# Attention and MoE on one core: where the loads of v stand in the queue, and which pairs take k and v in runs

## The chip, the cores and the metric

One core of one Trainium2 chip (trn2) runs the whole program. The metric is the device time of one execution in microseconds (us). The times of a kernel are the median of several executions; the profile is one further execution, taken by the hardware profiler.

## The reference

The kernel computes an attention layer and feeds its output to a feed-forward layer with a gate (called MoE below). q, k and v are float32 of shape (4, 8, 576, 64): batch, heads, tokens, head dimension.

```python
q_rot, k_rot = rotate(q), rotate(k)            # rotary embedding, halves of 32
scores = q_rot @ k_rot.T / sqrt(64)
attn = exp(scores - max) / (sum + 1e-9)
x = attn @ v                                   # to (4, 576, 512)
h = relu(x @ w_in)                             # 512 -> 1024
gate = sigmoid(conv over tokens of h, 3 taps)  # per channel
out = (h * gate) @ w_out                       # 1024 -> 512
```

w_in and w_out arrive as 64-bit floats and are turned into float32 on the chip.

## The kernel before

The 32 heads are worked on as 16 pairs of heads (p = 0 to 15). A pair has 5 steps (`STEPS = 5`): four for 128 queries each of both heads, and one for the remaining 64 queries of both. Step number n = 5p + s runs over 0 to 79; below, "pair p's first step" is step 5p. Steps 0 to 25 (`WIDE = 26`) have wide score tiles and no MoE work; while they run, VectorE also converts the weights. From step 26 on MoE units are interleaved with the steps, and what is left of the MoE comes behind the last step.

The work of a pair: `load` brings q and k (four DMAs each, tiles rq and rk), `rope` turns them on GpSimd (L203 and L206), `emit_TQ` transposes them on VectorE into qT and kT (L247, L251 to L254), `emit_S` makes the scores on TensorE into PSUM (tile sp, L278 and L304), VectorE takes the negated row maximum (negm, L286), ScalarE the exponential (st, and str for the fifth step, L290), TensorE transposes it (tp, L338), ScalarE copies it to pt (L212), and `emit_E` (L410) multiplies it with v (vm for keys 0 to 511, vr for the last 64). `load_v` brings vm and vr. The sums are inverted (`emit_rinv`, tile rt), sent to DRAM in four small DMAs (rd, L389) and read back, spread over partitions, in three DMAs (rb, L395 to L397, in `emit_rb`). Three steps later VectorE scales the pair's output with it (xn, L424). That result is written to xT by a DMA for the first token blocks (L434). The pieces of the weights come by DMA L650 and are sent back into winl by DMA L683.

Order. Nothing is scheduled by a tool: `at(n, rank, fn)` puts a piece of work into a plan, and the plan is emitted step by step, by rank within a step. Every engine carries out its own list in that order. All DMAs but four are issued by SyncE (SP), one after the other. So a DMA that has to wait, for a buffer or for its semaphore, holds all those behind it. The DMAs of SP carry eight semaphores in turn, and each issue waits for the earlier DMA on its semaphore, the eighth before it, to have landed.

Two forms of loading ("runs"). Where `runs(p)` holds, a partition takes 18 tokens that lie in a row in DRAM, so that a piece of k is 4,608 bytes and one of v 1,024 bytes; the angles for k then come from a second table, tabk, and v is brought in 12 DMAs. Otherwise the pieces are 256 bytes, the angles come from tabt, and v is brought in 4 DMAs. Before the change `runs(p)` holds for p = 1 to 6.

Memory. tabk lies in a pool that is closed at step 26. The pool of the MoE tiles rr takes that place, and the first thing done with rr is a memset on VectorE of its two edge columns (L842).

Places in the plan, with n = 5p: q and k of a pair are loaded at steps n-9 and n-7 (rank 16), rope comes at n-6 (rank 18), the transposes at n-4 and n-2, rd of the pair at n+5 (rank 4.5), rb at n+6 (rank 17) in the wide part, the scaling xn at n+8 and n+9, and v at n+1 (rank 19, L776).

Of the kernel before, what the change touches and what calls it, by code (L numbers as in the profile page):

```python
# [20 lines left out]
def attention_moe_kernel(ctx, tc, q, k, v, w_in, conv_w, w_out, tab, tabx, out):  # L21
# [13 lines left out]
    STEPS = 5  # L35
# [108 lines left out]
    def load(p, part):  # L144
        b, hp = divmod(p, NPB)
        x = raw[p, part] = p1.tile([128, S // 32, 2, 32], F32, tag="r" + part, name="r" + part)
        for h in range(2):
            y = (q if part == "q" else k)[b, 2 * hp + h]
            y = y.rearrange("(i c) d -> i c d", i=32) if part == "k" and runs(p) else y.rearrange("(c i) d -> i c d", i=32)
            for g in range(2):  # L150
                r = slice(64 * h + 32 * g, 64 * h + 32 * g + 32)
                nc.sync.dma_start(out=x[r].rearrange("i c e d -> i c (e d)"), in_=y)
# [1 line left out]
    vmain = {}  # L154

    def runs(p):
        return 0 < p and STEPS * p - 7 < WIDE - 2

    def load_v(p):
        if p < 2:  # L160
            nc.vector.memset(vrem[p], 0.0)
        b, hp = divmod(p, NPB)
        t = vmain[p] = p1.tile([128, 2, 4, D], F32, tag="vm", name="vm", bufs=2)
        for h in range(2):
            if runs(p):
                y = v[b, 2 * hp + h].rearrange("(i c) d -> i c d", i=32)
                for c in range(4):
                    nc.sync.dma_start(out=t[32 * c:32 * c + 32, h], in_=y[:, 4 * c:4 * c + 4])
                for c in range(2):
                    r = slice(64 * h + 32 * c, 64 * h + 32 * c + 32)  # L170
                    nc.sync.dma_start(out=vrem[p % 2][r, h, :], in_=y[:, 16 + c])
            else:
                nc.sync.dma_start(out=t[:, h], in_=v[b, 2 * hp + h, 0:512, :].rearrange("(t p) d -> p t d", p=128))
                nc.sync.dma_start(out=vrem[p % 2][64 * h:64 * h + 64, h, :], in_=v[b, 2 * hp + h, 512:S, :])
# [23 lines left out]
    def rope(p, part):  # L198
        x = raw[p, part]
        tb = tabk[0].rearrange("p (c e d) -> p c e d", e=2, d=32) if part == "k" and runs(p) else tabt  # L200
        for a in range(0, 18, 3):
            y = x[:, a:a + 3]
            nc.gpsimd.tensor_tensor(out=y, in0=y, in1=tb[:, a:a + 3], op=ALU.mult)  # L203
        for a in range(0, 18, 6):
            y = x[:, a:a + 6]
            nc.gpsimd.tensor_tensor(out=y[:, :, 0, :], in0=y[:, :, 0, :], in1=y[:, :, 1, :], op=ALU.add)  # L206
# [36 lines left out]
    def emit_TQ(p, part):  # L243
        qk_tiles(p)
        x = raw.pop((p, part))[:, :, 0, :]
        if part == "q":
            nc.vector.transpose(out=QT[p].rearrange("p (c i) -> p c i", i=32), in_=x)  # L247
        else:
            kt = KT[p].rearrange("p (c i) -> p c i", i=32)
            if runs(p):  # L250
                nc.vector.transpose(out=kt[:, 2:18].rearrange("p (t c) i -> p t c i", t=4), in_=x[:, 0:16].rearrange("p (c t) d -> p t c d", t=4))  # L251
                nc.vector.transpose(out=kt[:, 18:20], in_=x[:, 16:18])
            else:
                nc.vector.transpose(out=kt[:, 2:20], in_=x)  # L254
            if p * STEPS < WIDE:
                for h in range(2):
                    r = slice(64 * h, 64 * h + 64)
                    nc.vector.transpose(out=krem[p % 2][r, r].rearrange("p (c i) -> p c i", i=32), in_=x[r, 16:18])
            if p * STEPS + STEPS > WIDE:
                nc.vector.transpose(out=kt[:, 0:2], in_=x[:, 16:18])  # L260
# [467 lines left out]
    WIDE = 26  # L728
# [14 lines left out]
    def at(n, rank, fn):  # L743
        plan.setdefault(n, []).append((rank, len(plan.get(n, [])), fn))

    def emit():
        with tc.manual_schedule(engines=engines):
# [20 lines left out]
            for p in range(1, NP):  # L768
                n = STEPS * p
                early = n - 10 >= WIDE - 1  # L770
                for i, part in enumerate("qk"):
                    if p > 1:
                        at(max(n - 10, WIDE) if early else n - 9 + 2 * i, 19.6 if early else 16, lambda p=p, part=part: load(p, part))
                    at(n - 8 + i if early else max(n - 6, 0), 18, lambda p=p, part=part: rope(p, part))
                    at(n - 5 + i * (n - 15 < WIDE) if early else max(n - 4 + 2 * i, 2), 0.45, lambda p=p, part=part: emit_TQ(p, part))
                at(n + 1, 19, lambda p=p: load_v(p))  # L776
            for p in range(NP):
                n = STEPS * p
                for s in range(STEPS):
# [47 lines left out]
            n = -1  # L827
# [41 lines left out]
            for u in seq + second + m2_units(t, B * S // 128):  # L869
                u()  # L870
                tick()

    emit()


# [50 lines left out]
```

## Time and profile before

| | |
|---|---|
| median of 3 runs | 492.11 us (488.82 to 492.88) |
| the profiled execution | 492.34 us |
| its span, first to last instruction | 490.5 us |
| outside the span | 1.84 us |
| TensorE (PE) busy | 457.9 us, 93% of the span |
| VectorE (DVE) busy | 357.2 us, 73% |
| ScalarE (ACT) busy | 328.2 us, 67% |
| GpSimd (POOL) busy | 293.6 us, 60% |
| mean granted TensorE clock | 0.989 of full speed |

How to read it: times count from the first instruction of the span. A row of the timeline gives the start, the time taken, the engine, the line and the tiles; in square brackets stands how long the engine was idle just before and what it is thought to have waited for. PEld is TensorE's loading of weights. SPq is the queue of SyncE. The chain of waits follows the work that ended last back to the start; a DMA in it stands with its issue and the time until it released something, that is, its landing. Busy matmuls are modelled, so a stretch with PE busy throughout may still hold some slack.

### The profile page before, as it was taken

Reading aid. Unit: us, or ns where it says so; the run is one execution under the profiler, and the core shown is the slowest. Engines: PE = TensorE matmul, PEld = TensorE weight load, DVE = VectorE, ACT = ScalarE, POOL = GpSimd, SP = SyncE. Lnnn points to the kernel's source line nnn. Section 1 sums busy time; section 2 is a strip of 40 time slices with the busy share of each in tenths; the row PEclk is TensorE's granted clock in tenths of the full one; section 3 lists DMA queues with packets and bytes.
Section 4 is the critical chain, followed back from the end, with each engine's and each line's share of the span. In section 5 each row is a group of like instructions: output and inputs, shape, how many; then the busy total and the mean of one; then the engine's idle time right before and its main releaser. Section 6 shows DMA issues by size and latency. Waiting matters only on the chain.

```text
span 490.5 us, 12284 instructions
## 1 busy us (share of the span) xinstructions
PE 457.9 (93%) x4508; PEld 358.4 (73%) x4508; DVE 357.2 (73%) x646; ACT 328.2 (67%) x943; POOL 293.6 (60%) x479
## 2 busy tenths in 40 slices
PE   1888859989999999999999999999999999999997
PEld 1345536556686787878779787879797978899986
DVE  5598969993789987767768687877674665467931
ACT  1687757884979787785869686868686864244510
POOL 3838475988299969497885758483821313234520
PEclk9999988998999999999999999999999999999999
DMA  9888779556538090812709090909020200100011
GB/s 199 271 170 211 216 158 249 157 107 184 99 68 140 9 155 13 132 38 53 106 16 154 24 146 12 156 15 156 12 62 12 60 13 26 43 24 21 1 59 49
DMA packets 90591, 46.59 MB, mean 95 GB/s; under 512 B 77708, under 2 KB 83364, under 8 KB 90532
## 3 DMA queue, kind: packets, MB, share of 16 engines
q1 hardware_dynamic: 89188, 45.42, 42.5%
q8 instruction: 36, 0.59, 0.6%
q10 hardware_dynamic: 1344, 0.39, 0.4%
q14 instruction: 23, 0.19, 0.1%
HBM read 37.71 MB, written 4.79 MB: 87 GB/s over the span
## 4 chain that ended last, share of the span: by engine, by line
PE 68%; DVE 11%; DMA 7%; ACT 5%; POOL 3%; SPq 3%; issue 2%; ACTq 0%; DVEq 0%; POOLq 0%
PE sp L278 11%; PE mt L565 10%; PE pm L410 9%; PE pm L474 9%; PE pm L585 9%; PE mt L474 7%; PE tp L338 5%; PE pm L464 4%; DVE negm L286 3%; ACT st L290 2%; POOL rk L203 2%; DMA w<-moe_w_in 1%; PE sp L410 1%; DVE wf L630 1%; DVE wt L625 1%
## 5 line engine op out<-in xcount | busy, mean ns | idle before, releaser
L286 DVE TENSOR_REDUCE negm<-sp 128x1 f32<-128x576 f32 x144 | 102.5, 748 | 25.5 <-PE sp L278 16.2
L290 ACT ACTIVATE st<-sp,negm 128x576 f32<-128x576 f32 x128 | 93.7, 740 | 33.9 <-DVE negm L286 32.7
L278 PE MATMUL sp<-kT,qT 64*128 64x288 f32 (+4 forms) x556 | 99.7, 461 | 3.9 <-DVE kT L251 1.9
L212 ACT ACTIVATE pt<-tp 128x512 f32<-128x512 f32 (+3 forms) x176 | 84.3, 532 | 6.0 <-PE tp L338 5.6
L494 DVE SCALAR_TENSOR_TENSOR c<-rr,cw,c 128x288 f32<-128x288 f32 x128 | 78.7, 615 | 4.2
L203 POOL TENSOR_TENSOR rq<-rq,tabt 128x192 f32<-128x192 f32 x90 | 60.7, 707 | 26.6 <-DMA rq<-q 26.5
L512 POOL TENSOR_TENSOR gm<-c,gm 128x288 fp32r<-128x288 f32 (+4 forms) x72 | 45.7, 640 | 49.2 <-ACT gm L511 47.9
L278 PEld LDWEIGHTS sp<-kT,qT 64*128 64x128 f32 (+1 forms) x556 | 46.7, 177 | 27.4 <-issue 9.7
L338 PEld LDWEIGHTS tp<-idf,st 64*128 64x128 f32 x1024 | 42.1, 139 | 20.6 <-ACT st L290 9.5
L338 PE MATMUL tp<-idf,st 64*128 64x64 f32 x1024 | 48.2, 227 | 5.4 <-ACT st L290 4.7
L431 POOL TENSOR_TENSOR xT<-xn,xT 128x290 fp32r<-128x290 f32 x24 | 20.3, 846 | 52.9 <-ACT xT L427 52.8
L410 PE MATMUL pm<-pt,vm 128*64 128x290 f32 x368 | 50.0, 411 | 0.4 <-ACT pt L212 0.4
L585 PE MATMUL pm<-wouth,gm 64*128 64x256 f32 x512 | 49.5, 281 | 0.0
L474 PE MATMUL pm<-xT,winh 128*128 128x290 f32 x224 | 47.1, 304 | 0.0
L503 DVE SCALAR_TENSOR_TENSOR c<-c,rr 128x288 f32<-128x288 f32 x64 | 38.7, 625 | 10.3 <-ACT c L500 10.2
L492 DVE TENSOR_SCALAR c<-rr,cw 128x288 f32<-128x288 f32 x56 | 26.3, 470 | 23.3 <-ACT rr L484 23.0
L585 PEld LDWEIGHTS pm<-wouth,gm 64*128 64x128 f32 x512 | 42.8, 185 | 0.0
L410 PEld LDWEIGHTS pm<-pt,vm 128*64 128x64 f32 x368 | 27.6, 136 | 16.1 <-ACT pt L212 1.1
L585 PE MATMUL pm<-woutl,gm 64*128 64x256 f32 x256 | 39.0, 276 | 0.0
L500 ACT ACTIVATE c<-c 128x288 f32<-128x288 f32 x64 | 28.5, 445 | 12.2 <-DVE c L494 12.2
L474 PEld LDWEIGHTS pm<-xT,winh 128*128 128x128 f32 x224 | 35.8, 189 | 0.9
L464 PE MATMUL pm<-xT,winl 128*128 128x290 f32 x128 | 34.5, 417 | 0.0
(122 smaller groups left out, 978.0 us busy)
## 6 DMA issues: line engine op xcount, KB each, us to landing
rq<-q SPq DMA_DIRECT2D x60, 144.0 KB
rk<-k SPq DMA_DIRECT2D x60, 144.0 KB
w<-moe_w_in SPq DMA_DIRECT2D x8, 512.0 KB
w<-moe_w_out SPq DMA_DIRECT2D x8, 512.0 KB
vm<-v SPq DMA_DIRECT2D x20, 128.0 KB
rb<-rd SPq DMA_DIRECT2D x16, 144.0 KB
out<-oh SPq DMA_DIRECT2D x18, 128.0 KB
winl<-wf SPq DMA_DIRECT2D x8, 256.0 KB
```

Of the source, the lines that this page charges most:

```text
L203: nc.gpsimd.tensor_tensor(out=y, in0=y, in1=tb[:, a:a + 3], op=ALU.mult)
L212: nc.scalar.activation(out=out, in_=in_, func=AF.Copy, scale=1.0 if sc is None else sc)
L278: nc.tensor.matmul(out=out, lhsT=qt[64 * h:64 * h + 64, c], rhs=kt[64 * h:64 * h + 64, a:a + n], start=True, stop=True)
L286: reds.setdefault((p, s), []).append(lambda: nc.vector.tensor_reduce(out=nm, in_=sc, axis=AX.XY if len(sc.shape) == 3 else AX.X, op=ALU.ma ...
L290: lambda: nc.scalar.activation(out=dst, in_=sc, func=AF.Exp, bias=nm, scale=1.0, accum_out=sm)
L338: nc.tensor.transpose(ps[r][:, 64 * k:64 * k + 64], x[i], idf[i, i])
L410: nc.tensor.matmul(out=xp[64 * h:64 * h + 64, :], lhsT=vmain[p][:, h, i, :] if i < 4 else vrem[p % 2][:, h, :], rhs=pt[:, 2 * i + h if i < ...
L464: nc.tensor.matmul(out=ps[:, 0:XW], lhsT=winl[:, kk, fs].bitcast(F32), rhs=xT[:, xslot[b, kk, j], j, :].bitcast(F32), start=(kk == 0), sto ...
L474: nc.tensor.matmul(out=ps[:, 0:XW], lhsT=w[:, kk, fs], rhs=xT[:, xs, e, :], start=(i == 0), stop=(i == n - 1))
L494: nc.vector.scalar_tensor_tensor(out=c, in0=r[:, j + e:j + e + HS], scalar=cw[:, 8 * e + f:8 * e + f + 1], in1=c, op0=ALU.mult, op1=ALU.add,)
L565: nc.tensor.matmul(out=ops[tt][:, 0:width], lhsT=g_tile(tt, f, e), rhs=w[:, f, cols], start=(f == 0 and i == 0), stop=(f == NF - 1 and i = ...
L585: nc.tensor.matmul(out=ps[r][:, 0:256], lhsT=g_tile(tt, f, e)[rows], rhs=w[rows, f, cols], start=(f == 0 and i == 0), stop=(f == NF - 1 an ...
```

## The change

`runs(p)` holds for p = 1 to 5 instead of 1 to 6: pair 6, whose scores are steps 30 to 34, takes k and v in 256-byte pieces and its angles from tabt. And v of a pair is issued at step n-1 with rank 15 instead of step n+1 with rank 19, for every pair from 1 to 15.

```diff
     def runs(p):
-        return 0 < p and STEPS * p - 7 < WIDE - 2
+        return 0 < p and STEPS * p < WIDE
...
-                at(n + 1, 19, lambda p=p: load_v(p))
+                at(n - 1, 15, lambda p=p: load_v(p))
```

First place, SyncE's list between two weight pieces at steps 4 to 6; w is a weight piece, winl the piece that is sent back, rd and rb belong to pair 0, rq to pair 3, vm and vr to pair 1. Before:

```order
L650 DMA w_372<-moe_w_in 128x512
L683 DMA winl<-wf 128x512
L650 DMA w_428<-moe_w_in 128x512
L389 DMA rd<-rt 9x32 x4
L683 DMA winl<-wf 128x512
L152 DMA rq<-q 32x18x64 x4
L395 DMA rb<-rd 64x576
L396 DMA rb<-rd 64x512
L397 DMA rb<-rd 64x64
L168 DMA vm<-v 32x256 x4
L171 DMA vr_82<-v 32x64 x2
```

The 12 DMAs of v (8 of vm, 4 of vr) stand behind rb. With the change, w_442 being the piece that was w_428:

```order
L650 DMA w_372<-moe_w_in 128x512
L168 DMA vm<-v 32x256 x4
L171 DMA vr_82<-v 32x64 x2
L168 DMA vm<-v 32x256 x4
L171 DMA vr_82<-v 32x64 x2
L683 DMA winl<-wf 128x512
L650 DMA w_442<-moe_w_in 128x512
L389 DMA rd<-rt 9x32 x4
L683 DMA winl<-wf 128x512
L152 DMA rq<-q 32x18x64 x4
L395 DMA rb<-rd 64x576
```

The same 12 now stand behind the weight piece w_372 and in front of rd, rq and rb. The eighth of them carries the semaphore of w_372, which before was next carried by the first DMA of rq.

Second place, VectorE's list at step 26, with waits; rt are the inverted sums of pair 4, rr the MoE tiles, negm the row maxima of step 26. Before:

```order
L386 STREAM_TRANSPOSE rt_1608<-rvc_0_78 128x32 [waits DMAHW0_49,DVE_49]
L842 MEMSET rr0_1637 128x2 [waits Pool_49]
L842 MEMSET rr1_1638 128x2
L842 MEMSET rr2_1639 128x2
L842 MEMSET rr3_1640 128x2
L286 TENSOR_REDUCE negm_1540<-sp_1656 128x1 [waits PE_49]
```

With the change:

```order
L386 STREAM_TRANSPOSE rt_1621<-rvc_0_78 128x32 [waits DMAHW4_49,DVE_49]
L842 MEMSET rr0_1650 128x2
L842 MEMSET rr1_1651 128x2
L842 MEMSET rr2_1652 128x2
L842 MEMSET rr3_1653 128x2
L286 TENSOR_REDUCE negm_1540<-sp_1669 128x1 [waits PE_49]
```

The order is the same; the first memset no longer waits for GpSimd.

Third place, GpSimd's list where rope of pair 6 stands:

```order
 L203 TENSOR_TENSOR rq<-rq,tabt 128x192 x6
 L206 TENSOR_TENSOR rq<-rq 128x6x32 x3
-L203 TENSOR_TENSOR rk<-rk,tabk 128x192 x6
+L203 TENSOR_TENSOR rk<-rk,tabt 128x192 x6
 L206 TENSOR_TENSOR rk<-rk 128x6x32 x3
```

The rope of pair 6 reads tabt in place of tabk; nothing moved on GpSimd.

## Rows read from the trace of the kernel before

**Rows 1.** Windows of 10 us: engines' busy time and instructions, clock, DMA share.

```profile
core 0: us, PE busy (x) PEld busy (x) DVE busy (x) ACT busy (x) POOL busy (x), PEclk, DMA share, GB/s
...
90.00:100.00 10.00, 8.82 (x104) 5.60 (x100) 9.52 (x17) 8.38 (x24) 8.29 (x14) 1.00 0.61 161
...
130.00:140.00 10.00, 10.00 (x85) 7.65 (x85) 9.03 (x18) 9.93 (x30) 6.72 (x11) 1.00 0.80 147
...
290.00:300.00 10.00, 10.00 (x126) 7.76 (x127) 8.12 (x13) 8.03 (x25) 10.00 (x16) 1.00 0.21 51
```

**Rows 2.** Timeline of VectorE and TensorE in steps 8 to 15.

```profile
47.54 0.86 DVE L424 TENSOR_TENSOR xn<-xn,rb 128x290 f32<-128x290 f32 x1 [0.98 <-DMA rb<-rd]
49.97 0.96 DVE L630 SCALAR_TENSOR_TENSOR wf<-w,wt 128x512 int32<-128x512 int32 x1
49.99 0.52 PE L338 MATMUL tp<-idf,str 64*128 64x64 f32 x10 [1.78 <-ACT str L290]
...
66.10 0.71 DVE L251 STREAM_TRANSPOSE kT<-rk 128x512 f32<-128x512 f32 x1 [1.05 <-POOL rk L206]
69.92 0.85 DVE L424 TENSOR_TENSOR xn<-xn,rb 128x290 f32<-128x290 f32 x1 [2.61 <-DMA rb<-rd]
72.36 0.80 PE L338 MATMUL tp<-idf,str 64*128 64x64 f32 x10 [3.74 <-ACT str L290]
...
77.93 1.42 DVE L286 TENSOR_REDUCE negm<-sp 128x1 f32<-128x576 f32 x2 [0.80 <-PE sp L410]
```

**Rows 3.** Timeline of SyncE's queue, steps 4 to 13: start, time taken to issue.

```profile
32.26 0.35 SPq L650 DMA_DIRECT2D w<-moe_w_in  x1
...
36.77 1.75 SPq L389 DMA_DIRECT2D rd<-rt  x4
...
39.95 3.02 SPq L152 DMA_DIRECT2D rq<-q  x4
43.08 0.48 SPq L395 DMA_DIRECT2D rb<-rd  x1
...
44.88 1.97 SPq L168 DMA_DIRECT2D vm<-v  x4
...
49.72 0.89 SPq L171 DMA_DIRECT2D vr<-v  x2
...
54.81 1.63 SPq L650 DMA_DIRECT2D w<-moe_w_out  x1
...
64.58 0.48 SPq L395 DMA_DIRECT2D rb<-rd  x1
```

**Rows 4.** Chain of waits: start, length until something was released.

```profile
34.99 6.91 DMA w<-moe_w_in
...
65.11 4.72 DMA rb<-rd
```

**Rows 5.** Windows of 2 us around two idle times of TensorE, columns as in rows 1.

```profile
48.00:50.00 2.00, 0.22 (x4) 0.02 (x2) 1.97 (x4) 0.90 (x4) 2.00 (x4) 1.00 0.20 55
...
72.00:74.00 2.00, 1.64 (x14) 1.04 (x14) 1.97 (x5) 1.44 (x7) 2.00 (x3) 0.50 0.17 44
```

**Rows 6.** Timeline of VectorE, TensorE and GpSimd around step 26.

```profile
115.67 1.24 PE L278 MATMUL sp<-kT,qT 64*128 64x288 f32 x8
...
122.14 1.70 PE L278 MATMUL sp<-kT,qT 64*128 64x288 f32 x7
...
125.10 0.39 PE L375 MATMUL pm<-idf,st 64*128 64x64 f32 x2 [0.53 <-ACT pt L212]
...
120.45 0.06 DVE L842 MEMSET rr<- 128x2 f32 x1 [7.30 <-POOL rk L203]
...
133.28 4.25 POOL L203 TENSOR_TENSOR rq<-rq,tabt 128x192 f32<-128x192 f32 x6 [9.22 <-DMA rq<-q]
...
151.16 1.71 PE L278 MATMUL sp<-kT,qT 64*128 64x288 f32 x7 [0.96 <-ACT st L290]
```

**Rows 7.** Waits of SyncE's queue over the span: us in total, times, longest.

```profile
SPq L389 <- DVE rt L386: 83.4, 12, 10.8
```

## The prediction

> **What bounds the kernel now.** I read the windows first. In steps 16 to 25 (90 to 100 us) VectorE is the busiest engine, 9.52 of 10 us, and TensorE has gaps. From 130 us on TensorE is busy without a gap, and in the long stretch that 290 to 300 us stands for it is 10.00 [rows 1]. So a gain must come from a place where VectorE or TensorE stands still before about 165 us. The timeline then names these places. At 47.54 and 69.92 VectorE waits for rb, the inverted sums that come back from DRAM (0.98 and 2.61 us), at 66.10 for the rope of pair 3's k (1.05); TensorE runs dry behind each scaling (1.78 and 3.74 us) [rows 2]. At step 26 VectorE stands still for 7.30 us in front of a memset of 0.06 us, for the rope that reads tabk [rows 6]. Who is late is read from SyncE's queue: it issues almost without a pause, and the 12 DMAs of v take from 44.88 to 50.61, 5.73 us, 0.48 each [rows 3]. The chain shows how long landings take under load: 6.91 us for a weight piece, 4.72 for rb [rows 4].
>
> **The first part: v moves in front of rd, rq and rb.** The queue does the same work per pair; what counts is who now stands behind the 5.73 us.
>
> Pair 1's v, steps 4 to 6. The eighth of its DMAs needs the semaphore of the weight piece issued at 32.26. Before, the first DMA of rq had that place, and it started at 39.95 [rows 3]; nothing in front of it has changed, so the eighth starts then. Five DMAs from there are 2.4 us (42.35). Behind them come winl (0.48, priced as the issue of rb), the weight piece (0.35), rd (1.75), winl (0.48) and rq. For rq I have 3.02 with its waits, or 4 x 0.48 = 1.92 without. The first rb starts at 47.3 to 48.4 instead of 43.08: 4.2 to 5.3 later. The most is reached if the third DMA of rq has to wait for a weight piece that again takes 6.91: issued at about 42.9, landed at 49.8, rb at 50.8, or 7.7 later. The least is reached if rb, in a queue thinned by then, lands faster by 1.3 than before: 2.9 later. I take 4.5, near the low end, because the weight piece is now issued behind small DMAs and not behind other weights. VectorE was already waiting there, so its scaling moves from 47.54 by the full 4.5, and TensorE's 1.78 us becomes 6.3.
>
> What is regained. v no longer stands between rb and pair 3's k, so that k comes 5.73 - 4.5 = 1.2 us earlier by the clock, 5.7 earlier as seen from the delayed VectorE; the wait of 1.05 goes. What is late next is the second rb. VectorE reaches that scaling at 69.92 - 2.61 = 67.31 before; now at 67.31 + 4.5 - 1.05 = 70.76. SyncE must first issue the weight piece of 54.81, whose buffer comes free with the conversion that ends at 49.97 + 0.96 = 50.93 [rows 2]; shifted by 4.5, that is 55.4. Then, at issue prices: 0.35, v 5.73, winl and xT 0.96, rd 1.75, weights and winl 0.83, rq 1.92, together 11.5: rb starts at 66.9 instead of 64.58. If all the waits of before stay (64.58 - 54.81 = 9.77, plus 5.73), it starts at 70.9. I take 67.1, near the low end, since the long landings in between have the 5.73 us of small DMAs to finish in. The time from the first rb's issue to landing was 65.11 + 4.72 - 64.58 = 5.25 [rows 3, 4]; the scaling starts at 72.4, 2.5 later than before. This absorbs what came earlier: **+2.5**, with ends of 70.76 - 69.92 = +0.8 and 70.9 - 64.58 = +6.3.
>
> Pairs 2 to 5: VectorE has no wait for SyncE's loads that the trace puts above 0.2 us between 78 and 113 us, and is nearly full [rows 1]; delayed by 2.5 us it gives the queue that much more room. Cost 0; without that room each later rb could be late as the second one is, which is a rival below. From pair 6 on SyncE waits for the inverted sums for 83.4 us in 12 pieces [rows 7]; v is issued in front of such a wait and its buffer has long been read. Cost 0, gain 0. The memset of vr moves by one step on VectorE: 0.
>
> TensorE's clock. After the 3.74 us idle the granted clock stands at 0.50, its lower level of 1.2 GHz; in the stretch with the 1.78 us idle it is 1.00 [rows 2, 5]. An idle time of 6.3 us at step 8 will bring a second such stretch. The price in the first was 0.80 us, for which VectorE waited at 77.93 for TensorE [rows 2]; here it lies in front of the second rb, for which VectorE waits longer anyhow (72.4 - 70.76 = 1.6), so I cost it at 0, and at 0.8 if that cover is gone. The Trainium skill, "TensorE: Matmul & The Clock Gate", Part 1, says that an engine left idle falls back to half its clock and gets it back by sustained work; the trace agrees (0.50 against 1.00), and by the page alone the sum would be 0.8 higher.
>
> **The second part: pair 6 out of the runs.** The memset at step 26 loses its wait of 7.30 us. VectorE's next work is the reduction of step 26's scores, which TensorE has finished at 115.67 + 1.24 = 116.91; it began at about 120.5. So VectorE gains at most 3.55 us there. TensorE, which is the bound from here on, lost less: 0.53 at 125.10, 0.46 in the score matmuls at 122.14 (1.70 against 1.24, and one of eight was still missing), and 0.96 at 151.16 [rows 6]. The last of these hangs on GpSimd, idle for 9.22 us until pair 7's q landed; the v of pair 5 that stood in front of that q is now two steps earlier, so q comes up to 5.73 us sooner. Sum **-1.95**. Ends: 0, if TensorE's work only closes up elsewhere, and -3.55, all of VectorE's gain. What is late next is TensorE itself. The other edits of pair 6 cost nothing: v in 4 DMAs instead of 12, in the long wait [rows 7]; k in 256-byte pieces lands later, but GpSimd has its 9.22 idle us right behind that rope.
>
> **Sum.** 2.5 - 1.95 = +0.55 on the profiled execution's 492.34 is 492.9. The median of the runs is 0.23 lower (492.11), so 492.7.
>
> **Rivals** (each less the 0.23).
> A. The issues cost little, and rb stays on time: then only gains remain, 1.05 and 1.95: 489.1. For it: the 1.75 and 3.02 of rd and rq contain waits in which v could be issued. Against it: the eighth DMA of v cannot start before 39.95. The Trainium skill, "DMA: Bandwidth & Descriptors", "Issuing engines are not separate DMA queues", calls a sequencer's time to start a DMA usually small beside the DMA itself; the rows of v (0.48 each, 12 in 5.73 us) do not agree here, and by that rule the sum would be this rival's.
> B. Slower: the limit of eight DMAs in flight decides. v's small DMAs queue behind weight pieces at both places, all old waits stay, and the second rb starts at 70.9: +6.3, with nothing gained at step 26: 498.4. It decides from the point where rb lands more than about 3 us behind the arrival of VectorE. For it: 6.91 us landings. Against: v's own landings are short and give the weights time.
> C. The change doesn't do what it says: another reader of the freed memory holds the memset, and VectorE still stands: 492.34 + 2.5, so 494.6. Against: the changed list shows no wait there.
> D. VectorE and not TensorE paces 113 to 165 us: 3.55 instead of 1.95 is gained, 491.1; with the full 7.30 it would be 487.3. For it: 9.03 of 10 at 130 us. Against: TensorE at 10.00 [rows 1].
>
> **How the numbers follow.** Forecast 0.54, A 0.14, B 0.16, C 0.06, D 0.10. About 1% (4.9 us, so below 487.2 or above 497.0) is what a measurement can tell from no change. Faster than that needs the far ends of A and D together: 0.08. Slower is nearly all of B: 0.15. The rest, 0.77, lies within. The range runs from below A to near B's end, 488 to 498; the forecast alone would be 490 to 496.
>
> **What would show it.** Right: a wait for rb of some 5 us before the first scaling at about 52, a lower clock after it, no wait at kT of pair 3, a second scaling at about 72.4, no gap before the memset at step 26, GpSimd's wait of 9.22 shorter by some 5 us, and TensorE without gaps from 125 to 165. Wrong: the first rb issued before 46; a wait for rb at pairs 2 or 3; or a step 26 that comes more than 3 us earlier or 5 us later than before.

## The result and the profile after

| | before | changed |
|---|---|---|
| median of 12 runs | 491.74 us (488.82 to 493.08) | 496.44 us (495.13 to 499.48) |
| the profiled execution | 492.34 us | 497.58 us |
| its span | 490.5 us | 495.4 us |

The changed kernel is slower by 1.0%: the ratio is 1.0103, with a 95% interval of 1.0081 to 1.0126. The medians differ by 4.7 us.

The head of the profile's page first: TensorE and VectorE have the work they had, so the time went into waits.

```profile
PE 458.0 (92%) x4508; PEld 357.8 (72%) x4508; DVE 358.7 (72%) x645; ACT 327.8 (66%) x943; POOL 294.8 (60%) x479
```

VectorE's timeline answers to [rows 2] and [rows 6]; columns as there.

```profile
53.48 0.56 DVE L424 TENSOR_TENSOR xn<-xn,rb 128x290 f32<-128x290 f32 x1 [7.10 <-DMA rb<-rd]
...
70.80 0.69 DVE L251 STREAM_TRANSPOSE kT<-rk 128x512 f32<-128x512 f32 x1
...
77.42 0.78 DVE L424 TENSOR_TENSOR xn<-xn,rb 128x290 f32<-128x290 f32 x1 [5.42 <-DMA rb<-rd]
...
97.06 0.46 DVE L424 TENSOR_TENSOR xn<-xn,rb 128x290 f32<-128x290 f32 x1 [0.34 <-DMA rb<-rd]
...
120.83 0.21 DVE L386 STREAM_TRANSPOSE rt<-rvc 128x32 f32<-128x32 f32 x1
121.00 0.09 DVE L842 MEMSET rr<- 128x2 f32 x4
124.61 1.42 DVE L286 TENSOR_REDUCE negm<-sp 128x1 f32<-128x576 f32 x2 [3.52 <-PE sp L278]
```

The waits for rb have grown from 0.98 and 2.61 us to 7.10 and 5.42. The wait at kT of pair 3 is gone (no bracket at 70.80), and so is the 7.30 in front of the memset; but the next reduction then waits 3.52 us for TensorE.

TensorE's timeline, the same stretches:

```profile
55.63 0.80 PE L338 MATMUL tp<-idf,str 64*128 64x64 f32 x10 [7.94 <-ACT str L290]
79.79 0.80 PE L338 MATMUL tp<-idf,str 64*128 64x64 f32 x10 [5.96 <-ACT str L290]
```

The idle times of 1.78 and 3.74 [rows 2] are now 7.94 and 5.96. Between 120 and 162 us there is none over 0.2 us; the 0.53 and 0.96 of [rows 6] have gone.

SyncE's queue, which answers to [rows 3]:

```profile
31.53 0.35 SPq L650 DMA_DIRECT2D w<-moe_w_in  x1
31.92 5.56 SPq L168 DMA_DIRECT2D vm<-v  x4
37.58 0.89 SPq L171 DMA_DIRECT2D vr<-v  x2
38.71 3.35 SPq L168 DMA_DIRECT2D vm<-v  x4
42.10 0.88 SPq L171 DMA_DIRECT2D vr<-v  x2
...
48.84 0.48 SPq L395 DMA_DIRECT2D rb<-rd  x1
...
56.62 0.35 SPq L650 DMA_DIRECT2D w<-moe_w_out  x1
...
70.79 1.22 SPq L395 DMA_DIRECT2D rb<-rd  x1
```

The 12 DMAs of pair 1's v, 5.73 us before, now take from 31.92 to 42.98, 11.1 us: in both groups of four the queue stands, and the eighth DMA starts at 39.94. The waits of that queue name most of the reason, 4.8 of the 5.3 us that the group takes longer: DMAs whose semaphore comes round again have not landed yet, two weight pieces and one winl.

```profile
SPq L168 <- DMA w<-moe_w_in: 3.1, 2, 2.2
...
SPq L168 <- DMA winl<-wf: 1.7, 1, 1.7
```

The windows show what a standing queue does to the transfers; columns as in [rows 1]. First before, then changed:

```profile
36.00:48.00 12.00, 11.33 (x136) 7.58 (x134) 10.43 (x19) 9.98 (x26) 10.20 (x16) 1.00 0.87 225
48.00:54.00 6.00, 3.53 (x40) 2.18 (x38) 5.93 (x9) 3.04 (x10) 5.25 (x8) 1.00 0.43 128
```

```profile
36.00:48.00 12.00, 11.22 (x134) 7.46 (x134) 9.79 (x17) 9.83 (x26) 8.52 (x13) 1.00 0.54 156
48.00:54.00 6.00, 0.00 (x0) 0.00 (x0) 0.52 (x2) 0.00 (x0) 1.41 (x3) 0.74 1.09 226
...
54.00:56.00 2.00, 0.37 (x6) 0.37 (x8) 1.97 (x4) 1.18 (x4) 2.00 (x3) 0.50 1.08 283
...
80.00:82.00 2.00, 2.00 (x14) 0.83 (x12) 2.00 (x5) 1.01 (x4) 2.00 (x3) 0.50 0.81 172
```

From 36 to 48 us the DMA share falls from 0.87 to 0.54, since the queue does not get to issue; from 48 to 54 it rises from 0.43 to 1.09, while TensorE does nothing at all. Behind both idle times the granted clock is 0.50, its lower level.

So the delay against before, read at the end of each pair's sums (rt, L386), is 0 at pair 0 (35.6 against 35.7), 6.0 at pair 1 (61.1, 55.1), 8.6 at pair 2 (85.5, 76.9), 7.9 at pair 4 (120.8, 112.9), and then only 6.6 at pair 5 (150.4, 143.8) and 4.9 at pair 6 (173.6, 168.7). It stays at 4.9 to the end. Two questions follow: what makes the 7.9 us, and what gives 3.0 back.

### The profile page after: what moved, and what is told of

It is laid out like the page before. It is cut to its first block, busy times and chain, and to the rows that moved or that the text cites. A ratio compares the mean times of both kernels' runs of the same rounds, so it can differ in the third digit from the quotient of the medians.

```text
span 495.4 us, 12269 instructions
## 1 busy us (share of the span) xinstructions
PE 458.0 (92%) x4508; PEld 357.8 (72%) x4508; DVE 358.7 (72%) x645; ACT 327.8 (66%) x943; POOL 294.8 (60%) x479
## 4 chain that ended last, share of the span: by engine, by line
PE 66%; DVE 14%; ACT 9%; DMA 4%; issue 2%; SPq 2%; POOL 2%; ACTq 0%; DVEq 0%
PE sp L278 10%; PE mt L565 10%; PE pm L410 9%; PE pm L474 9%; PE pm L585 9%; PE mt L474 7%; PE tp L338 5%; DVE negm L286 5%; PE pm L464 4%; ACT st L290 4%; DMA rb<-rd 3%; ACT pt L212 2%; DVE c L494 1%; SPq L152 1%; DVE wt L620 1%
## 5 line engine op out<-in xcount | busy, mean ns | idle before, releaser
L431 POOL TENSOR_TENSOR xT<-xn,xT 128x290 fp32r<-128x290 f32 x24 | 21.0, 877 | 52.9 <-ACT xT L427 52.8
L492 DVE TENSOR_SCALAR c<-rr,cw 128x288 f32<-128x288 f32 x56 | 26.2, 469 | 23.1 <-ACT rr L484 23.0
L203 POOL TENSOR_TENSOR rk<-rk,tabt 128x192 f32<-128x192 f32 x60 | 37.7, 663 | 0.0
```

## The experiments

Each ratio is against the kernel before on the same chip: 492.79 us in the first four runs, 492.12 in the next four, 492.02 in the last four. Medians are of 12 runs, but those of e1, e3 and e4 of 6 and that of e12 of 8. "Pair 4 to pair 6" is the time between the rt of these two pairs: 55.8 us before, 52.8 in the changed kernel.

### The two parts alone

e1: v moved, pair 6 still in runs.

```diff
-                at(n + 1, 19, lambda p=p: load_v(p))
+                at(n - 1, 15, lambda p=p: load_v(p))
```

> The move of v alone; pair 6 stays in runs. Theory 1 (the two parts add: the earlier v costs about 7.5 us at the first two scalings, the lost wait at step 26 gives about 3): first scaling near 53.5, second near 77.4, the 7.30 us gap in front of the memset at step 26 is back or partly back, total 499.0 to 499.6 (7.5 above 491.7). Theory 2 (the 3 us that the changed kernel got back between steps 26 and 35 are slack that any delay uses up there, not the removed wait): total 496.4, as the changed kernel.

Measured: 496.62 us, ratio 1.0073 (1.005 to 1.0095). Delay 7.5 at pair 4 (rt at 120.4), 4.5 at pair 6 (173.2). The memset, at 124.58, still waits for GpSimd (3.95 us), and the 3 us come back all the same (pair 4 to pair 6: 52.8). So the loss and what comes back belong to the move of v, and not to the second part; of the two theories the second came.

e2: pair 6 out of the runs, v at its old place.

```diff
-        return 0 < p and STEPS * p - 7 < WIDE - 2
+        return 0 < p and STEPS * p < WIDE
```

> Pair 6 out of the runs alone; v stays at its old place. Theory 1: first scaling 47.5 and second 69.9 as before, no gap at the memset, total 488.7 (3 below 491.7). Theory 2: no gap at the memset either, but TensorE was the bound there and nothing comes of it: 491.7.

Measured: 493.45 us, ratio 1.0017 (0.9993 to 1.0041). The memset stands at 113.07 without a wait, and nothing is gained: pair 4 to pair 6 take 57.6 us. TensorE's timeline shows the waits that stand there now, one for xT and one in front of the scores of a step of pair 6, for ScalarE's exponential:

```profile
119.31 0.76 PE L464 MATMUL pm<-xT,winl 128*128 128x290 f32 x2 [1.65 <-DMA xT<-xn]
151.70 2.53 PE L278 MATMUL sp<-kT,qT 64*128 64x288 f32 x7 [2.46 <-ACT st L290]
```

Some 4 us earlier VectorE, on whose row maximum that exponential waits, stood for GpSimd's rope of pair 7's k. The same transpose before, in e2 and in the changed kernel:

```profile
147.54 0.78 DVE L254 STREAM_TRANSPOSE kT<-rk 128x576 f32<-128x576 f32 x1 [1.58 <-POOL rk L206]
```

```profile
148.08 0.78 DVE L254 STREAM_TRANSPOSE kT<-rk 128x576 f32<-128x576 f32 x1 [3.22 <-POOL rk L206]
```

```profile
152.23 0.77 DVE L254 STREAM_TRANSPOSE kT<-rk 128x576 f32<-128x576 f32 x1
```

### Which pair pays

e3: as the changed kernel, but pair 1's v at its old place.

```diff
-                at(n - 1, 15, lambda p=p: load_v(p))
+                at(*((n + 1, 19) if p <= 1 else (n - 1, 15)), lambda p=p: load_v(p))
```

> The change, but pair 1's v at its old place; pairs 2 to 15 stay moved. Theory A (each v in front of rd delays its own rb): first scaling back at 47.5, second scaling still late, rb starts at 66.3 to 69 instead of 64.6, the scaling at 72 to 74.5; total 491 to 493.3. Theory B (only the crowded queue of steps 4 to 8 delays rb, and the second delay is its echo): both scalings as before, total 488.7.

Measured: 496.03 us, ratio 1.0064 (1.0039 to 1.0088).

```profile
46.85 0.85 DVE L424 TENSOR_TENSOR xn<-xn,rb 128x290 f32<-128x290 f32 x1 [0.54 <-DMA rb<-rd]
...
77.43 0.89 DVE L424 TENSOR_TENSOR xn<-xn,rb 128x290 f32<-128x290 f32 x1 [10.37 <-DMA rb<-rd]
```

The first scaling is back, but the second is as late as in the changed kernel, and later than I expected (72 to 74.5): rb is issued at 71.63, against 70.79 in the changed kernel, though VectorE was not held up in front of it. So the second wait is no echo of the first.

e4: the same with pairs 1 and 2 at the old place (`p <= 2`).

> The change, but v of pairs 1 and 2 at the old place; pairs 3 to 15 stay moved. Theory A (the places of pairs 3 to 5 cost nothing, since rb there has room): both scalings as before, total 488.7, the same as with the runs alone. Theory C (the places of pairs 3 to 5 are worth something by themselves, either way): the wait for rb at the scaling near 89 grows to 3 us or more, total 491.5 or more, or the total falls clearly below that of the runs alone.

Measured: 495.99 us, ratio 1.0065 (1.0043 to 1.0087).

```profile
69.69 0.75 DVE L424 TENSOR_TENSOR xn<-xn,rb 128x290 f32<-128x290 f32 x1 [2.74 <-DMA rb<-rd]
...
93.83 0.46 DVE L424 TENSOR_TENSOR xn<-xn,rb 128x290 f32<-128x290 f32 x1 [4.57 <-DMA rb<-rd]
```

Now the third scaling waits, which in the changed kernel waits 0.34: theory C. In e3 and e4 the first pair with the moved v makes the rb behind it late, and the next scalings wait 0.7 us at most; only in the changed kernel and e1, where pair 1's v is moved, do two rb in a row come late. Pair 4 to pair 6 take 52.1.

### What the price consists of

e5: the changed kernel, but v of a pair in runs brought in 4 DMAs instead of 12, with the same pieces in memory (later lines have numbers lower by 3).

```diff
-                for c in range(4):
-                    nc.sync.dma_start(out=t[32 * c:32 * c + 32, h], in_=y[:, 4 * c:4 * c + 4])
-                for c in range(2):
-                    r = slice(64 * h + 32 * c, 64 * h + 32 * c + 32)
-                    nc.sync.dma_start(out=vrem[p % 2][r, h, :], in_=y[:, 16 + c])
+                nc.sync.dma_start(out=t[:, h], in_=y[:, 0:16].rearrange("i (c j) d -> c i j d", c=4))
+                nc.sync.dma_start(out=vrem[p % 2][64 * h:64 * h + 64, h, :], in_=y[:, 16:18].rearrange("i c d -> c i d"))
```

> The changed kernel, but a pair in runs takes v in 4 DMAs instead of 12, with the same pieces of 1,024 and 512 bytes. Theory A (what delays rb is the issue of 12 DMAs and the eight semaphores they pass): 1.9 us of issues instead of 5.7, and the fourth DMA reaches no weight piece's semaphore; first scaling near 48.5, second at 70 or earlier, total 3 to 6 us below the changed kernel, 490.5 to 493.5. Theory D (what delays rb is that v's bytes lie in front of it in the DMA engines, however they are issued): first scaling near 53, second near 77, total as the changed kernel, 496.5.

Measured: 489.82 us, ratio 0.997 (0.9943 to 0.9998).

```profile
33.79 0.64 SPq L167 DMA_DIRECT2D vm<-v  x1
...
36.73 0.53 SPq L168 DMA_DIRECT2D vr<-v  x1
...
46.25 0.49 SPq L392 DMA_DIRECT2D rb<-rd  x1
...
65.74 1.12 SPq L392 DMA_DIRECT2D rb<-rd  x1
```

```profile
50.81 0.63 DVE L421 TENSOR_TENSOR xn<-xn,rb 128x290 f32<-128x290 f32 x1 [4.74 <-DMA rb<-rd]
...
71.51 0.50 DVE L421 TENSOR_TENSOR xn<-xn,rb 128x290 f32<-128x290 f32 x1 [1.93 <-DMA rb<-rd]
```

```profile
36.00:48.00 12.00, 11.10 (x134) 7.37 (x134) 9.95 (x17) 9.83 (x26) 8.39 (x13) 1.00 0.86 216
```

v takes 3.5 us of the queue instead of 11.1, rb of pair 1 is issued 5.0 us earlier than in the changed kernel (65.74 against 70.79), and the DMA share from 36 to 48 us is back at 0.86. The bytes are the same, so it is the number of issues and the eight semaphores that hold the queue, not the transfers; how much belongs to the issues and how much to the semaphores was not separated. The first scaling is still 3.3 us later than before; I had expected 1. Even so the time is a little below the 490.5 to 493.5 of theory A. In ratios, 8 issues fewer per pair are worth 1.0103 - 0.997, or 1.3%. The Trainium skill, "DMA: Bandwidth & Descriptors", "Issuing engines are not separate DMA queues", calls the time that it takes to start a DMA usually small relative to the DMA itself; for 12 small DMAs in a row these runs do not bear that out.

e6: the same 4 DMAs with v at its old place and pair 6 out of the runs.

> Pair 6 out of the runs, v at its old place, v of a pair in runs in 4 DMAs instead of 12. Theory A: k of pairs 3 to 5, and through it all later issues, come up to 3.8 us earlier, the wait for kT near 66 goes and the wait for rb near 70 shrinks from 3 us to 1 or less; total 1 to 3 us below the kernel before, 489 to 491. Theory D: nothing moves, 492.8.

Measured: 490.78 us, ratio 0.998 (0.9949 to 1.0011), against 1.0017 with 12 DMAs. The wait for kT near 66 us has gone, as expected; the one for rb is still 2.40 (at 68.95), where I had expected 1 or less. So of e5's 1.3% about 0.4% is had at the old place too, and some 0.9% only at the new one, both uncertain by 0.3% or more. Pair 4 to pair 6 take 55.6: what comes back does not come from fewer issues.

### What gives 3 us back

e7: as the changed kernel, pairs 1 to 4 at the old place (`p <= 4`), 12 DMAs.

> The change, but v of pairs 1 to 4 at the old place; only pairs 5 to 15 are moved. Theory E (the about 3 us that every kernel with a moved v gets back between 121 and 173 us come from pair 5's v no longer standing in front of pair 7's q): the stretch from the inverted sums of pair 4 to those of pair 6 takes 52 to 53 us instead of 55.8, total 3 below the kernel before, 489.5. Theory F (they are got back only because a delayed VectorE leaves the queue more room): the stretch takes 55 or more, total 492 to 493.

Measured: 491.97 us, ratio 1.0003 (0.998 to 1.0026); pair 4 to pair 6 take 55.1. TensorE again waits for xT (1.23 at 118.65). Theory E, with pair 5's v alone, has failed; theory F has the number, but e10 below shows the 3 us without a delayed VectorE.

e8: as e7, with pair 6 in runs.

> As the run before, with pair 6 in runs as before the change. Theory E: also 489.5 to 490.5, so that the part with the runs is worth at most 1 us; the memset at step 26 waits as before, up to 7 us, without an effect on TensorE. If the two parts need each other (the memset's wait counts only once pair 7's q is early): 491.5 or more, 2 above the run before.

Measured: 490.99 us, ratio 0.9982 (0.9959 to 1.0005); pair 4 to pair 6 take 54.9. The memset waits 7.26 us at 119.74, and TensorE's idle time there is 0.53 as before.

e9: the kernel before, with the memset given to GpSimd. Every other engine's list is unchanged; it was meant to take away VectorE's wait alone.

```diff
-                        nc.vector.memset(t[:, 0:XW + 1:XW], 0.0)
+                        nc.gpsimd.memset(t[:, 0:XW + 1:XW], 0.0)
```

> The kernel before with the four edge memsets of step 26 given to GpSimd instead of VectorE; loads, runs and order else as before. So VectorE loses its 7.30 us wait, and nothing else changes. Theory of the prediction (the wait is worth 1.95 us on the path): step 26's inverted sums stay at 112.9, those of pair 6 come at 166.8 instead of 168.7, and the time is 1.95 us under the kernel before. Theory now (TensorE is the bound there, the wait is idle time of an engine that is not it): VectorE waits for TensorE's scores instead, pair 6's sums stay within 0.7 us of 168.7, and the time is that of the kernel before within 0.7 us. Rival D (VectorE paces the stretch): 3.5 us or more under.

Measured: 492.44 us, ratio 1.0007 (0.9985 to 1.003). VectorE, ScalarE and TensorE at step 26 and behind it:

```profile
115.04 1.42 DVE L286 TENSOR_REDUCE negm<-sp 128x1 f32<-128x576 f32 x2 [2.22 <-PE sp L278]
...
122.87 1.42 DVE L286 TENSOR_REDUCE negm<-sp 128x1 f32<-128x576 f32 x2 [4.66 <-PE sp L278]
```

```profile
123.55 0.41 ACT L484 ACTIVATE rr<-pm 128x289 f32<-128x289 f32 x1 [5.19 <-POOL rr L842]
```

```profile
118.32 0.76 PE L464 MATMUL pm<-xT,winl 128*128 128x290 f32 x2 [0.95 <-DMA xT<-xn]
...
125.00 0.39 PE L375 MATMUL pm<-idf,st 64*128 64x64 f32 x2 [1.67 <-ACT pt L212]
```

VectorE now waits 2.22 and 4.66 us for TensorE's scores in place of the 7.30. But the wait at the memset has not gone, it has moved: on GpSimd the memset stands behind the rope, at 123.42, and ScalarE, whose next work writes rr, waits 5.19 us for it. TensorE's 0.53 has become 1.67 behind that ScalarE work, 0.95 for xT is new, and pair 6's sums come at 169.2 against 168.7. So e9 does not say by itself what the wait is worth. Three pairs of kernels that differ in pair 6's form alone do. With and without the wait, the stretch from pair 4 to pair 6 takes 54.9 and 55.1 us (e8 with 7.26 us of wait, e7 with none), 52.8 and 52.8 (e1 with 3.95, the changed kernel) and, below, 51.9 and 51.8 (e12 with 4.49, e5): the wait at the memset is worth nothing there.

### Keeping the gain without the price

e10: v in 4 DMAs, pairs 1 and 2 at the old place, pairs 3 to 15 at the new one, pair 6 out of the runs.

> v of every pair in 4 DMAs; v of pairs 1 and 2 at the old place, of pairs 3 to 15 at the new one; pair 6 out of the runs. Theory (each moved v delays the first rb behind it, by its issue time; the room that the queue gains behind it is worth 3 us between steps 25 and 35): the first two scalings at 47 and 69 as in the kernel before, the third delayed by at most 2 us, pair 4's sums at 111 to 113, pair 6's 52 to 53 us later, and a time of 488 to 489.5, below the changed kernel with v in 4 DMAs (489.8). Rival (the slack is used up by other waits, such as that for xT): pair 4 to pair 6 take 55 us as in the kernels with v at the old place, and the time is 490.5 to 491.

Measured: 489.19 us, ratio 0.9961 (0.9937 to 0.9984). First scalings at 46.4, 67.8 and 89.0, none later than before; pair 4 to pair 6 take 51.8.

e11: the same with pair 6 in runs.

> As the run with v in 4 DMAs and pairs 3 to 15 moved, but with pair 6 in the runs as before. If pair 6's form of loading is worth nothing, the same time within 0.7 us; if the 256-byte pieces cost something in the queue, up to 1 us less; by the prediction's term it would be 1.95 us more.

Measured: 489.62 us, ratio 0.9942 (0.9919 to 0.9965); pair 4 to pair 6 take 52.1. The same time as e10, and not 1.95 us more.

e12: the changed kernel with v in 4 DMAs (e5) and pair 6 in runs.

> The changed kernel with v in 4 DMAs and with pair 6 in the runs as before. Against the same with pair 6 out of the runs (489.8): the same within 0.7 us if that part is worth nothing; 1.95 us more by the prediction's term; about 1 us less if the small pieces of k cost something. First scaling at 50.8, second at 71.5 in all these cases.

Measured: 488.0 us, ratio 0.9934 (0.9901 to 0.9967). The scalings come at 49.3 and 70.5, 1.0 to 1.5 us earlier than I expected; pair 4 to pair 6 take 51.9. The memset waits, and yet TensorE hardly stands still; its busy time comes first in the windows of that stretch, before and in e12:

```profile
117.24 0.06 DVE L839 MEMSET rr<- 128x2 f32 x1 [4.49 <-POOL rk L200]
```

```profile
112.90:168.70 55.80, 53.79 (x430) 38.75 (x429) 43.78 (x77) 44.22 (x126) 44.90 (x69) 0.98 0.49 102
```

```profile
112.50:164.40 51.90, 51.49 (x422) 34.17 (x418) 44.83 (x76) 43.36 (x126) 42.99 (x66) 1.00 0.47 95
```

TensorE stands still for 2.0 us of it before (55.80 - 53.79) and for 0.4 in e12. That is 1.6 of the 3.9 us; the rest is in busy time (53.79 against 51.49), of which the lower clock before (mean 0.98) makes about 1 us, an estimate from the two means. What the rest of it is was not found.

Over all kernels: where v of pair 4 is moved (the changed kernel, e1, e3, e4, e5, e10, e11, e12), the stretch from pair 4 to pair 6 takes 51.8 to 53.4 us; where it isn't (before, e2, e6, e7, e8, e9), 54.9 to 57.6. In all the kernels of the first group pair 3's v is moved too, so pair 4 alone is not shown. The form of pair 6, the number of DMAs and the memset's wait do not sort the kernels in this way.

What does sort them is the arrival of pair 7's q. GpSimd starts its rope 19.8 to 21.4 us after pair 4's sums in the second group (before: 133.28 against 112.94, or 20.3), and 15.0 to 15.7 after them in the first. The row of the changed kernel, where the sums come at 120.83; the bracket names VectorE as the last of several that the rope waited for:

```profile
136.49 4.12 POOL L203 TENSOR_TENSOR rq<-rq,tabt 128x192 f32<-128x192 f32 x6 [7.72 <-DVE negm L286]
```

And VectorE waits for pair 7's k, whose rope comes behind that of q, in all six kernels of the second group (0.48 to 3.22 us at that transpose, 1.58 before) and in none of the first. The chain of the kernel before goes this way, through v of pair 5, q and k of pair 7 and GpSimd; that of the changed kernel has no DMA and no GpSimd between 116 and 172 us:

```profile
126.40 0.42 SPq L168
...
128.26 2.99 DMA rq<-q
...
134.00 3.96 DMA rk<-k
...
141.90 3.75 POOL rk L203 x6
...
147.54 0.78 DVE kT L254
```

Why moving pair 5's v alone does not do it is seen in the queue: in e7 that v is issued from 114.28 on, after pair 4's sums (112.7), and still holds rd, rb and q; in the changed kernel from 118.84 on, before them (120.8). No run moves q of pair 7 by itself, so this rests on the traces.

e10, e11 and e12 are faster than before by 0.4 to 0.7%, and so faster than both kernels; from each other they can't be told apart. All of them keep the early v and give up the 12 issues.

## Why the prediction was right or wrong

The direction was right and the size was not: +0.55 us of working stands against +4.7 measured, at the very edge of "within 1%", above the forecast's own 490 to 496 and inside the range, whose upper end came from rival B. That the sign came out right is in part luck: both terms were too small, 7.9 us lost where 2.5 stood and 3.0 got back where 1.95 stood, and the second came from another cause for the most part. Of the rivals, B's mechanism decided at both places, though with 3 us back that B didn't have.

**Pair 1's v: right in its mechanism, short by 1.4.** The eighth DMA was to start at 39.95, and started at 39.94, held by the weight piece as said; that the two agree so closely is luck, since that piece was issued 0.73 us earlier than before (31.53 against 32.26). The first rb was issued 5.8 later, at 48.84, where I had taken 4.5 (ends 2.9 and 7.7), and the scaling began 4.64 us after that. The scaling came at 53.48 instead of 52.0, and TensorE's idle time was 7.94 instead of 6.3. The clock's fall behind it came, and the wait at kT of pair 3 went, both as forecast.

**The second rb: the step that failed.** "I take 67.1, near the low end, since the long landings in between have the 5.73 us of small DMAs to finish in." It was issued at 70.79; "if all the waits of before stay" had given 70.9. The queue took 14.2 us from the weight piece (56.62) to rb: 11.5 without waits, 15.5 with all of them, so most stayed; and the weight piece itself came 1.2 us later than the 55.4 that I had worked out. The scaling began 6.6 us after rb's issue, not 5.25, in a stretch with a DMA share of 1.07 (72 to 78 us). The picture of "a queue thinned by then" was wrong: the queue that stood from 32 to 43 us left the engines half empty and then brought everything at once. The term of +2.5 measured +7.5 at the scaling (77.42 against 69.92), and e3 shows that it is there without the first delay. The cover of the clock's price held: TensorE's slow stretch made VectorE wait 0.68 and 0.52 us at 64.92 and 68.39, but both lie in front of a longer wait for rb, so they cost nothing, as I said.

**Pairs 2 to 5 at 0: right, for the reason given.** Pair 2's rb came 0.34 us late where VectorE had been delayed, and 4.57 where it had not (e4). The condition "without that room each later rb could be late" is what e3 and e4 showed, each for the first rb behind a moved v.

**Pair 6 out of the runs, -1.95: wrong in its cause.** The wait went as said, and VectorE's 7.30 us were worth 0: with the wait gone and v at its old place the time is no shorter (e2: 1.0017), and e1 and e12 wait 3.95 and 4.49 us there and lose nothing by it. The end "0, if TensorE's work only closes up elsewhere" was the true one. Still, the three gaps of TensorE that made up the 1.95 did go in the changed kernel, and more with them, 3.0 us: the move of v did that (e1 against before). I had given v's move only the last of the three, by way of pair 7's q, which was to come up to 5.73 us sooner. That way was right: counted from pair 4's sums, its rope starts 4.7 us sooner (15.7 against 20.3). GpSimd's own wait shrank from 9.22 to 7.72 us only, since its work in front of it came sooner as well. But pair 5's v, to which I had put it down, does not do it alone (e7).

**What the small pieces cost** was put at 0. Five pairs of kernels differ in pair 6's form alone, and in all five the 256-byte form is the slower one, by ratios that differ by 0.002 to 0.004 (changed and e1, e2 and before, e7 and e8, e10 and e11, e5 and e12). None is clear by itself (and the medians of e10 and e11 stand the other way round); together they speak for about 1 us of cost, which stays unsettled.

**The rivals.** A fell: 12 issues cost much; with 4 of them (e5) the time is near A's 489.1. C fell: no wait in front of the memset. D fell with e2, where VectorE's wait is gone and nothing is gained. Of the signs that were to prove me wrong, two came: a step 26 more than 5 us later, and in e4 a wait for rb at pair 2.

## What to carry to other kernels

On one in-order queue a moved transfer is priced by how many issues it has and by which semaphore they wait for, at the first small transfer behind it that an engine is due to read; bytes come second. Merge the issues first, then move them.

A long idle time of an engine is worth only what the busiest engine loses through it: look for the gap in the busiest engine's own timeline, and if none ends with that wait, write 0. To test it, take the wait away, and then see that no other engine has taken it over: in e9 the memset went to GpSimd, and ScalarE waited in VectorE's place.

## What was not expected of the hardware

One VectorE instruction that scales rr (L492, 128x288) has two durations: in 9 of the 14 profiles, one of each kernel, one of its calls between 222 and 233 us takes 2.4 us, in the others none does. No edit sorts them cleanly: all five kernels with v in 4 DMAs have the long call, and of the nine others four. All calls of that line between 215 and 260 us, least, median and greatest time in ns, in the changed kernel and in e2:

```profile
L492 DVE TENSOR_SCALAR c<-rr,cw x6: 360/444/2441, 215.1 to 246.5; 128x288 f32<-128x288 f32 x6
```

```profile
L492 DVE TENSOR_SCALAR c<-rr,cw x7: 358/371/731, 215.1 to 258.7; 128x288 f32<-128x288 f32 x7
```

The steps from the rt of pair 7 to that of pair 9 take 56.3 to 58.0 us where the long call is (before: 195.5 to 253.2, or 57.7) and 55.4 to 55.9 where it isn't (e2: 197.7 to 253.1, or 55.4). So spans of two single profiles may differ by 2 us in a place far from the edit, and a small edit is read from the stretch that it touches and from the medians. Why the call is long was not found, nor whether it changes between executions of one kernel, which have one profile each.
